# A fused attention and two-expert kernel: the second expert's first product by Strassen's scheme, the gain folded into its second weights, and the order of all steps made anew

## The chip, the cores and the metric

The kernel runs on one core of one Trainium2 chip. The metric is the device time of one execution in microseconds (us), lower is better. Before the change the median of three runs is 810.53 us (810.01 to 811.58).

## The reference

Three stages follow each other: causal attention for 4 batches of 8 heads (576 positions, 64 wide), then two feed-forward experts over the 2304 tokens that attention gives (model width 512).

```
cum  = cumsum(max(s, 0));  bias = -(cum[i] - cum[j])
scores = q @ k.T / sqrt(64);  scores = where(causal, -1e9, scores + min(bias, 0))
x  = softmax(scores) @ v                       # (2304, 512), heads side by side
h  = x @ w_in1;  g = h - tanh(h)               # expert 1: 512 -> 2048
x2 = g @ w_out1                                # 2048 -> 512
h  = x2 @ w_in2                                # expert 2: 512 -> 1024
e  = exp(h - max(h));  solu = h * e / (sum(e) + 1e-9)
ln = (solu - mean) / sqrt(var + 1e-6) * g_ln   # mean, var over the 1024 columns
out = ln @ w_out2                              # 1024 -> 512
```

## The kernel before

**Matrix products.** A float32 operand of the experts is split in two fp32r parts, a rounded one (hi) and the rest (lo), and each product is three matmuls on TensorE: hi x hi, lo x hi, hi x lo. A name that ends in h or l is such a part (`w2ih`, `w2il`). Weights arrive as 64-bit floats; `split_w` turns 512 columns of 128 rows into hi and lo: one load on SyncE's queue (tile `cd`), an absolute value (L408, ScalarE), four VectorE instructions (L390, L393, L396, L401), a cast for hi and a subtraction for lo (L312 on VectorE, L313 on GpSimd).

**Attention.** Work is cut into jobs by pair of heads; the first four pairs are cut again, into a head job (rows 1 to 4 of 64 positions) and the rest. A job loads k, q, v (`kn`, `q`, `v`) and the running sums of s (`bc`); in the head jobs `bc` is loaded as s itself, raised at zero and scanned by VectorE (L551), in the others it comes from DRAM (`cum_d`), where one scan for all pairs (L474) has been stored. Scores (L655), their mask (L663), a minimum with the bias that also gives the row's least value (L672, custom VectorE instruction, tile `U`), the exponential (L683, ScalarE), the division (L687, mostly GpSimd), transposes (L721), the weighted sum of v (L761), a store to DRAM (`xd`).

**Expert 1** runs on 9 blocks of 256 tokens by 16 chunks of 128 hidden columns: L808 gives h (12 matmuls of 256 columns), L813 tanh, L817 g, L831 the second product. Chunks 0 to 3 and 4 to 7 go first (`VISITS`), mixed into attention, with partial sums kept in DRAM (`pd`); chunks 8 to 15 use weights that replace attention's buffers once it is over (about 400 us).

**Expert 2** runs per tile of 128 tokens, 18 tiles, in `expert2`: h by 24 matmuls of 512 columns (L925: two halves of 512 columns, four slices of 128 of the 512 inputs, three matmuls each) into the two-bank PSUM tile `big`; its maximum (L930), the exponential (L934), sum, h times e (L942), mean and variance (L947, L951), centring and gain in one VectorE instruction (L954, scalar_tensor_tensor with the broadcast tile `gain`), Newton steps for the root (L967 to L969, GpSimd), transposes (L975), splits (L288, L982), 24 matmuls (L989) and the scaling of the output (L994).

**Order.** All steps are in a list, and `ORDER` is a table written by hand: each word is a step and the engine that does it, `+n` stands for n matmuls on junk data (L498) that keep TensorE busy. `Plan.order` replays the table; each engine's queue, SyncE's DMA queue among them, runs in that order. `BUFS` gives the number of buffers per tile name. In the last part PSUM holds two `big` tiles (four banks) and four single banks `t`.

## Time and profile before

| What | Value |
| --- | --- |
| median of three runs | 810.53 us (810.01 to 811.58) |
| the profiled execution, its own time | 813.61 us |
| its span in the trace | 811.8 us |
| TensorE matmuls busy | 790.6 us, 97% of the span |
| VectorE, ScalarE, GpSimd busy | 505.0, 382.8, 159.3 us (62%, 47%, 20%) |
| DMA engines, moved in all | 112.43 MB, mean 138 GB/s |

The profiled execution took 1.8 us more than its span (start and end outside the engines' records) and 3.1 us more than the median. Busy shares are means over parts with different limits; a stretch by itself tells more. Matmul records overlap one another, so the length of one is longer than its distance from the next.

### The profile page before, as it was taken

Reading aid. Unit: us, or ns where it says so; the run is one execution under the profiler, and the core shown is the slowest. Engines: PE = TensorE matmul, PEld = TensorE weight load, DVE = VectorE, ACT = ScalarE, POOL = GpSimd, SP = SyncE. Lnnn points to the kernel's source line nnn. Section 1 sums busy time; section 2 is a strip of 40 time slices with the busy share of each in tenths; the row PEclk is TensorE's granted clock in tenths of the full one; section 3 lists DMA queues with packets and bytes.
Section 4 is the critical chain, followed back from the end, with each engine's and each line's share of the span. In section 5 each row is a group of like instructions: output and inputs, shape, how many; then the busy total and the mean of one; then the engine's idle time right before and its main releaser. Section 6 shows DMA issues by size and latency. Waiting matters only on the chain.

```text
span 811.8 us, 16663 instructions
## 1 busy us (share of the span) xinstructions
PE 790.6 (97%) x6320; PEld 697.1 (86%) x6320; DVE 505.0 (62%) x1368; ACT 382.8 (47%) x973; POOL 159.3 (20%) x344
## 2 busy tenths in 40 slices
PE   7798999999999999999999999999999999999998
PEld 5457677788898999999999989899998889998886
DVE  5776688884454388865589875617364643245773
ACT  4786888886656355543355432313222222232222
POOL 3343333441223000000010012302142110001211
PEclk9999999999999999999999999999999999999999
DMA  7996897886653589785655501102020101100101
GB/s 204 258 275 163 266 259 215 258 234 199 176 165 95 170 298 288 227 267 161 227 159 182 157 27 66 40 14 79 27 79 14 52 24 61 36 1 14 40 13 52
DMA packets 89137, 112.43 MB, mean 138 GB/s; under 512 B 10768, under 2 KB 73232, under 8 KB 89056
## 3 DMA queue, kind: packets, MB, share of 16 engines
q1 hardware_dynamic: 89056, 111.35, 45.6%
q8 instruction: 50, 0.82, 0.4%
q14 instruction: 31, 0.25, 0.1%
HBM read 87.63 MB, written 23.70 MB: 137 GB/s over the span
## 4 chain that ended last, share of the span: by engine, by line
PE 74%; DMA 10%; DVE 10%; ACT 3%; issue 2%; SPq 1%; POOL 0%; ACTq 0%; DVEq 0%; POOLq 0%
PE t L808 17%; PE big L925 12%; PE t L989 12%; PE big L831 10%; PE acc L831 8%; PE t L761 5%; PE t L721 5%; PE t L655 4%; DMA cd<-in_moe_w_in_dram 4%; DMA cd<-in_moe_w_out_dram 2%; DMA bc<-cum_d 2%; PE t L975 2%; DVE ct L401 2%; DVE ct L396 2%; ACT ct L408 1%
## 5 line engine op out<-in xcount | busy, mean ns | idle before, releaser
L808 PE MATMUL t<-xb,wih 128*128 128x256 f32 x1152 | 206.5, 281 | 0.6 <-DVE g L817 0.6
L808 PEld LDWEIGHTS t<-xb,wih 128*128 128x128 f32 x1152 | 177.2, 189 | 1.9 <-DVE g L817 0.8
L808 PE MATMUL t<-xb,wil 128*128 128x256 f32 x576 | 161.0, 280 | 0.0
L687 POOL TENSOR_SCALAR U<-U,r 128x256 f32<-128x256 f32 (+8 forms) x144 | 81.2, 577 | 147.9 <-DVE r L599 83.0
L808 PEld LDWEIGHTS t<-xb,wil 128*128 128x128 f32 x576 | 109.5, 190 | 0.0
L831 PE MATMUL big<-gh,woh 128*128 128x256 f32 x576 | 104.5, 282 | 2.3 <-ACT gh L288 1.2
L831 PE MATMUL acc<-gh,woh 128*128 128x256 f32 x576 | 104.9, 283 | 1.2 <-DVE gh L312 0.6
L817 DVE TENSOR_TENSOR g<-t,th 128x256 f32<-128x256 f32 x144 | 59.7, 420 | 58.9 <-ACT th L813 53.9
L831 PEld LDWEIGHTS big<-gh,woh 128*128 128x128 f32 x576 | 88.9, 188 | 4.8 <-DVE gh L312 2.3
L683 ACT ACTIVATE U<-U,m 128x64 f32<-128x64 f32 (+8 forms) x144 | 80.3, 559 | 26.1 <-DVE m L672 25.4
L312 DVE TENSOR_TENSOR gh<-g,gh 128x256 fp32r<-128x256 f32 x122 | 54.0, 445 | 59.1 <-ACT gh L288 44.0
L288 ACT CAST gh<-g 128x256 fp32r<-128x256 f32 x141 | 56.5, 405 | 71.6 <-DVE g L817 34.0
L831 PEld LDWEIGHTS acc<-gh,woh 128*128 128x128 f32 x576 | 88.2, 189 | 2.4 <-issue 1.3
L813 ACT ACTIVATE th<-t 128x256 f32<-128x256 f32 x144 | 54.6, 382 | 75.0 <-PE t L808 60.2
L925 PE MATMUL big<-w2ih,x 128*128 128x512 f32 x288 | 89.8, 393 | 0.0
L831 PE MATMUL big<-gh,wol 128*128 128x256 f32 x288 | 80.6, 280 | 0.0
L831 PE MATMUL acc<-gh,wol 128*128 128x256 f32 x288 | 80.4, 279 | 0.0
L672 DVE CUSTOM_DVE_ANT_0 U<-bc,t 128x384 f32<-128x384 f32 (+8 forms) x144 | 59.4, 443 | 13.4 <-PE t L663 7.8
L288 ACT COPY pt<-t 128x512 f32<-128x512 f32 (+4 forms) x160 | 60.1, 429 | 6.8 <-PE t L721 6.1
L967 POOL TENSOR_SCALAR u<-y,va 128x1 f32<-128x1 f32 x51 | 25.7, 503 | 190.6 <-DVE y L962 186.9
L313 POOL TENSOR_TENSOR gh<-g,gh 128x256 fp32r<-128x256 f32 x22 | 16.8, 767 | 235.2 <-ACT gh L288 151.4
L655 PE MATMUL t<-kn,q 64*64 64x288 f32 (+8 forms) x640 | 59.1, 420 | 1.6 <-DMA q<-in_q_dram 0.7
(99 smaller groups left out, 1384.6 us busy)
## 6 DMA issues: line engine op xcount, KB each, us to landing
xb<-xd SPq DMA_DIRECT2D x17, 1024.0 KB, 6.2
cd<-in_moe_w_in_dram SPq DMA_DIRECT2D x24, 512.0 KB, 4.6
cd<-in_moe_w_out_dram SPq DMA_DIRECT2D x24, 512.0 KB, 4.1
bc<-cum_d SPq DMA_DIRECT2D x32, 288.0 KB, 5.7
pd<-xp SPq DMA_DIRECT2D x18, 512.0 KB, 4.1
xp<-pd SPq DMA_DIRECT2D x18, 512.0 KB, 3.7
xd<-xs SPq DMA_DIRECT2D x16, 320.0 KB, 4.5
kn<-in_k_dram SPq DMA_DIRECT2D x16, 288.0 KB, 5.1
```

Of the source, the lines that this page charges most:

```text
L288: nc.scalar.copy(o, i)
L312: return self.any([("dve", t_dve(n, pair=True), lambda: nc.vector.tensor_tensor(*views(), op), "diff-dve"), ("pool", t_pool(n), lambda: nc ...
L655: nc.tensor.matmul(X[a][c, :z - a], lhsT=V["q"][r, o:o + 64], rhs=V["k"][r, a:z], start=True, stop=True, skip_group_check=True)
L672: nc.vector.tensor_tensor_reduce(out=X["u"][:, a:z], in0=V["bc"][:, n, a:z], in1=X[b][:, a - b:z - b], scale=-0.125, scalar=X["m"] if "m" ...
L683: nc.scalar.activation(out=X["u"][:, :nk], in_=X["u"][:, :nk], func=AF.Exp, scale=-1.0, bias=X["m"], accum_out=Y["s"][:, n:n + 1])
L687: eng.tensor_scalar(X["u"][:, :nk], X["u"][:, :nk], Y["r"][:, n:n + 1], 1.0, ALU.mult, ALU.mult)
L808: nc.tensor.matmul(ps, lhsT=w[l][:, k, f * 128:f * 128 + 128], rhs=xb[:, r, k, :], start=k == 0 and x == 0, stop=k == 3 and x == 2)
L813: nc.scalar.activation(out=X["th", f], in_=X["h", f], func=AF.Tanh)
L817: nc.vector.tensor_tensor(X["g", f], X["h", f], X["th", f], ALU.subtract)
L831: nc.tensor.matmul(X["acc"][:, m, :], lhsT=w[l][:, f, m * 128:m * 128 + 128], rhs=X["gh", f][:, r, :], start=f == c0 and m % 2 == 0 and x ...
L925: nc.tensor.matmul(X["h"][:, n, :], lhsT=self.x2[j][:, l, k, 128 * o:128 * o + 128], rhs=r[:, k, 512 * n:512 * n + 512], start=k == 0 and ...
L989: nc.tensor.matmul(X["po"], lhsT=X["lt", k // 4][:, l, k % 4, :], rhs=r[:, k, :], start=k == 0 and a == 0, stop=k == 7 and a == 2)
```

## The change

1. `expert2`'s first product goes over to a new function `products`, per block of 256 tokens: the 2 x 2 halves of tokens, inputs and hidden columns are multiplied by Strassen's scheme, with 7 products of 6 matmuls (128x512) instead of 8. Sums of x halves are made in `split_x2`, sums of weight quarters in `load_w2i`; five VectorE instructions and two copies put the products together. For the second tile of a block the two last of them are custom instructions that also give the row's least value, and h stands negated in `hc` in SBUF. The bank `b` is a pool of its own (`pc`), so three banks `t` are left.
2. g_ln is multiplied into `w2_out` when it is converted (`load_w2o`, one pass more); centring is then a tensor_scalar without the broadcast tile.
3. One exponential on a single column stands first in ScalarE's queue (`table`).
4. More buffers for attention and conversion, a second `cd`; x tiles alternate between two pools; some waits at the switch to the last part name other steps.
5. `ORDER` is another table throughout.

```diff
-BUFS = dict(junk=1, U=7, ps=6, bc=3, kn=4, q=4, v=3, pt0=2, pt1=2, xs=2, xb=2, th=2, g=2, gh=3,
-            acc=1, h2=1, xp=1, cd=1, ct=2, cu=1, e=2, o=1, x2=1)
+BUFS = dict(junk=1, U=9, ps=6, bc=4, kn=5, q=5, v=4, pt0=2, pt1=2, xs=3, xb=2, th=2, g=2, gh=3,
+            acc=1, h2=1, hb=1, hc=1, u2=1, xp=1, cd=2, ct=2, cu=1, e=2, o=1, x2=1)
-c 0 x f 4l 31u 89 3 i r u 4f 4i 31x 320 46 323 6 7u m o +38 10 1r 326 2f 9 36 13 19 1u 17 329 1x 86 20 4a 1c bu 1f 2i
+0 f x 3 i 10 l u 49 7x p 4i r +22 13 4l 1u 16 2i 86 1a 1c 1x 39 bu 2l 20 2p 6 1f 23 2r 1i 3c 89 1l 2u 4d 26 2x bx 4f
...
+        def table():
+            nc.scalar.activation(out=self.small("y"), in_=self.one, func=AF.Exp)
+
+        add("act", 1600, table, [self.one_ready], ahead=1.0e6)
...
+        h1 = self.copy(lambda: (view(0, 0, 2).rearrange("p s k f -> p (s k) f"), f1()), 512, False, [c1])
...
+        t1 = less("t1", "b12", "b11", [c1, c2])
+        t2 = less("t2", "b22", "t1", [t1])
+        t3 = less("t3", "b22", "b12", [c2])
+        t4 = less("t4", "b21", "t2", [t2, c2])
+        h3 = self.copy(lambda: (view(0, 3, 5), pair(n1())), 512, False, [t2])
+        l3 = self.diff(lambda: (view(1, 3, 5), pair(n1()), bits(view(0, 3, 5))), 512, [h3, t4, l1], rel=("ct",))
...
+        s1 = self.diff(lambda: (a(1, 1), a(1, 0), a(1, 1)), 256, [lb], op=ALU.add, split=350.0)
+        s3 = self.diff(lambda: (a(1, 0), a(0, 0), a(1, 0)), 256, [s1], split=350.0)
+        s2 = self.diff(lambda: (a(0, 0), a(1, 1), a(0, 0)), 256, [s3, la], split=350.0)
+        s4 = self.diff(lambda: (a(0, 1), a(0, 1), a(0, 0)), 256, [s2], split=350.0)
+        hc = self.copy(lambda: (four(0), sums()), 1024, False, [s4])
+        lc = self.diff(lambda: (four(1), sums(), bits(four(0))), 1024, [hc], rel=("xp",))
...
+                for k in range(2):
+                    for n, (l, r) in enumerate(((0, self.w2ih), (1, self.w2ih), (0, self.w2il))):
+                        nc.tensor.matmul(o, lhsT=self.x2[j][:, l, x, k], rhs=r[:, b, k, :], start=start and k == 0 and n == 0,
+                                         stop=k == 1 and n == 2, skip_group_check=True)
...
+        p1 = pe(product(0, 0, 0, True, True), [la], ("h2",))
+        p6 = pe(product(3, 4, None, True, True), [lc], ("hb",))
+        p5 = pe(product(6, 3, 1, True, True), [lc])
+        k1 = self.copy(keep1, 512, True, [p1], acq=("hc",))
+        u2 = add("dve", t_dve(512), sum2, [k1, p6], acq=("u2",))
+        k5 = self.copy(lambda: (c(1), Z["h"][:, 1]), 512, True, [p5, k1])
+        u4 = add("dve", t_dve(512), lambda: nc.vector.tensor_tensor(Z["h"][:, 1, :], Z["h"][:, 1, :], Z["u"], ALU.add), [u2, k5],
+                 rel=("u2",))
+        k15 = self.diff(lambda: (c(1), c(1), c(0)), 512, [k1, k5], op=ALU.add)
+        p2 = pe(product(1, 1, 0, False, True), [k1, la])
+        p3 = pe(product(4, 2, 1, False, True), [u4])
+        p7 = pe(product(5, 5, None, False, True), [u2])
+        c22 = add("dve", t_dve(512) + 34, lambda: second(1), [p7, k15])
+        p4 = pe(product(2, 6, None, False, True), [c22, lb], rel=("x2",))
+        c21 = add("dve", t_dve(512) + 34, lambda: second(0), [p4], rel=("hb",))
...
-            nc.vector.scalar_tensor_tensor(out=X["e"], in0=X["e"], scalar=X["mv"][:, 0:1], in1=self.gain,
-                                           op0=ALU.subtract, op1=ALU.mult)
+            nc.vector.tensor_scalar(X["e"], X["e"], X["mv"][:, 0:1], 1.0, ALU.subtract, ALU.mult)
...
-            self.ps = e(tc.tile_pool(name="pb2", bufs=4, space=PSUM))
+            self.ps = e(tc.tile_pool(name="pb2", bufs=3, space=PSUM))
+            self.pc = e(tc.tile_pool(name="pc", bufs=1, space=PSUM))
```

What the new order does is read from the instruction lists of both kernels. First SyncE's DMA queue from its start (`cd` is a weight chunk, `pt` the s of all pairs, `cum_d` its stored running sum). Before:

```order
L528 DMA v<-in_v_dram 128x2x128 x2
L381 DMA cd<-in_moe_w_in_dram 128x4x256
L528 DMA v<-in_v_dram 128x2x128
L455 DMA pt_131<-in_s_dram 32x576
L539 DMA bc<-in_s_dram 64x256 x2
L520 DMA kn<-in_k_dram 128x256
L524 DMA q<-in_q_dram 128x256
```

After:

```order
L586 DMA q<-in_q_dram 128x256
L590 DMA v<-in_v_dram 128x2x128
L601 DMA bc<-in_s_dram 64x256 x2
L582 DMA kn<-in_k_dram 128x256
L601 DMA bc<-in_s_dram 64x256 x4
L582 DMA kn<-in_k_dram 128x256
```

The first pair of k and q is complete with the fifth issue instead of the ninth; the weight chunk and the s of all pairs have moved behind them.

Second, TensorE's list where the first step of expert 1 stands (junk matmuls are L498 before, L560 after; scores' mask L663 and L725; transposes L721 and L783). Before, behind some 30 us of listed attention work:

```order
L663 MATMUL t<-mask,unit_64 64x64
L498 LDWEIGHTS junk
L498 MATMUL acc<-junk 128x256
L721 MATMUL t<-idx,U 128x128 x4
L721 MATMUL t<-idx,U 64x128
L721 MATMUL t<-idx,U 128x128 x2
L721 MATMUL t<-idn,U 128x128
L808 MATMUL t<-xb,wih_92 128x256 x2
```

After:

```order
L725 MATMUL t<-mask,unit_102 64x64
L560 LDWEIGHTS junk
L560 MATMUL acc<-junk 128x256
L783 MATMUL t<-idn,U 128x128 x3
L870 MATMUL t<-xb,wih_93 128x256 x2
```

The first step of expert 1 (L808, now L870) has moved from row 402 of TensorE's list to row 213. Junk matmuls are 80 in all before, 38 of them ahead of the first score; after they are 49, 22 of them ahead of the first score.

Third, TensorE's list at the products of expert 2. Before, at the first tile, they follow one another without a step of another engine between them:

```order
L808 MATMUL t<-xb,wil_4787 128x256
L925 MATMUL big<-w2ih,x_6671 128x512 x2
L925 MATMUL big<-w2il,x_6671 128x512
L925 MATMUL big<-w2ih,x_6671 128x512 x2
L925 MATMUL big<-w2il,x_6671 128x512
```

After, at the second block's last two products (both into `b`, which VectorE's c22 reads between them; L1127 is the output product, L989 before):

```order
L1011 MATMUL b<-w2ih,x_7203 128x512 x2
L1011 MATMUL b<-w2il,x_7203 128x512
L1127 MATMUL t<-w2oh,cd 128x512 x2
L1127 MATMUL t<-w2ol,cd 128x512
L1127 MATMUL t<-w2oh,cd 128x512 x2
L1127 MATMUL t<-w2ol,cd 128x512
L1011 MATMUL b<-w2ih,x_7203 128x512 x2
L1011 MATMUL b<-w2il,x_7203 128x512
```

Six matmuls of another step stand between the two products here; in five of the nine blocks it is six of 512 or twelve of 256 columns, in the others more.

## Rows read from the trace of the kernel before

**Rows 1.** Stretches of the span: stretch, sum; then PE, PEld, DVE, ACT, POOL busy us (instructions), PE clock, DMA share, GB/s.

```profile
0.00:20.00 20.00, 15.86 (x149) 10.93 (x149) 12.10 (x62) 9.63 (x33) 6.54 (x24) 1.00 0.74 205
20.00:40.00 20.00, 15.37 (x150) 9.29 (x151) 15.64 (x62) 15.63 (x48) 6.87 (x11) 1.00 1.03 253
40.00:60.00 20.00, 19.53 (x198) 12.07 (x195) 15.75 (x70) 17.02 (x51) 9.14 (x15) 1.00 1.06 280
60.00:80.00 20.00, 17.83 (x153) 13.90 (x154) 13.30 (x47) 14.20 (x43) 7.77 (x14) 0.91 0.67 166
80.00:100.00 20.00, 18.63 (x210) 13.67 (x201) 14.86 (x66) 15.45 (x48) 7.61 (x14) 1.00 0.87 265
400.00:420.00 20.00, 18.11 (x154) 17.51 (x153) 17.47 (x38) 10.57 (x24) 1.25 (x2) 1.00 0.54 158
420.00:440.00 20.00, 19.57 (x162) 18.58 (x161) 18.85 (x38) 10.85 (x23) 1.07 (x1) 1.00 0.62 192
440.00:460.00 20.00, 19.36 (x171) 19.16 (x170) 17.29 (x33) 10.58 (x25) 2.49 (x2) 1.00 0.62 196
460.00:740.00 280.00, 280.00 (x1829) 255.89 (x1828) 141.93 (x268) 78.70 (x163) 46.81 (x125) 1.00 0.12 38
```

**Rows 2.** The chain that ended last, its pieces in order of time: start us, length us, what.

```profile
5.18 2.64 DMA q<-in_q_dram
21.49 8.65 DMA bc<-cum_d
...
779.53 5.44 PE big L925 x24
```

**Rows 3.** Groups of TensorE instructions, the whole span: busy us, mean ns, then idle before.

```profile
L925 PE MATMUL big<-w2ih,x 128*128 128x512 f32 x288 | 89.8, 393 | 0.0
```

**Rows 4.** SyncE's DMA issues from the start: start us, us, line, tile, count.

```profile
0.74 0.96 SPq L528 DMA_DIRECT2D v<-in_v_dram  x2
...
3.31 1.20 SPq L539 DMA_DIRECT2D bc<-in_s_dram  x2
...
5.18 0.43 SPq L524 DMA_DIRECT2D q<-in_q_dram  x1
```

**Rows 5.** TensorE from the start: start us, us, line, tiles, count, [idle before and releaser].

```profile
1.10 6.03 PE L498 MATMUL acc<-junk 128*128 128x256 bf16 x38 [1.10 <-POOL junk L493]
7.87 0.33 PE L655 MATMUL t<-kn,q 64*64 64x64 f32 x4 [0.75 <-DMA q<-in_q_dram]
```

**Rows 6.** VectorE and ScalarE from the start, same columns.

```profile
7.99 1.35 DVE L474 TENSOR_TENSOR_SCAN pt<-one,pt 32x576 f32<-32x576 f32 x1
9.27 0.65 DVE L551 TENSOR_TENSOR_SCAN bc<-one,bc 128x256 f32<-128x256 f32 x1
10.43 0.20 DVE L672 CUSTOM_DVE_ANT_0 U<-bc,t 128x64 f32<-128x64 f32 x1
...
0.73 1.28 ACT L408 ACT_TABLE_LOAD   x1 [0.73 <-PEq L1144]
7.25 0.42 ACT L545 ACTIVATE bc<-bc 128x256 f32<-128x256 f32 x1 [0.57 <-DMA bc<-in_s_dram]
```

**Rows 7.** What TensorE waited for, 0 to 100 us: total us, times, longest us.

```profile
PE t L721 <- POOL U L687: 6.5, 7, 2.2
```

**Rows 8.** TensorE around 34 us and from 61 us, columns as in rows 5.

```profile
34.42 1.70 PE L498 MATMUL acc<-junk 128*128 128x256 bf16 x14
...
61.16 0.48 PE L808 MATMUL t<-xb,wih 128*128 128x256 f32 x2
```

**Rows 9.** Groups of VectorE and ScalarE instructions, by form: busy us, mean ns | idle before.

```profile
L954 DVE SCALAR_TENSOR_TENSOR ct<-ct,mv,gain 128x1024 f32<-128x1024 f32 x18 | 23.1, 1281 | 0.3
L390 DVE TENSOR_SCALAR ct<-ct 128x512 f32<-128x512 f32 x6 | 2.7, 443 | 1.1 <-ACT ct L408 1.1
...
L672 DVE CUSTOM_DVE_ANT_0 U<-bc,t 128x512 f32<-128x512 f32 x16 | 10.8, 672 | 0.7 <-PE t L663 0.3 <-PE t L655 0.2
...
L288 ACT COPY pt<-t 128x512 f32<-128x512 f32 x48 | 27.7, 590 | 2.9 <-PE t L721 2.6
```

More of the change, by code (lines that the diff above doesn't have):

```diff
@@ L341, in setup @@
         self.st.tile([128, 16], F32, name="pad_st", bufs=1)
+        self.gain = self.st.tile([128, 8], F32, name="gain", bufs=1)
         self.wes = ExitStack()
+        self.xo = self.wes.enter_context(tc.tile_pool(name="xo", bufs=1, side="left"))
         self.wa = self.w1_tiles(self.wes.enter_context(tc.tile_pool(name="wa", bufs=1, side="left")), 0, FA)
@@ L415, in split_w @@
                      [d], acq=("ct",))
+        if turn:
+            self.chain(turn + "d", d)
+            self.chain(turn, a)
         c = a
@@ L837, in expert1 @@
         else:
-            ld = self.dma(128 * 8192, load, list(ready), acq=("xb",), ahead=T["xb"],
+            ld = self.dma(128 * 8192, load, list(ready) + (list(deps) if j else []), acq=("xb",), ahead=T["xb"],
                           cost=650.0 * (1 + (j * TB // self.S != (j * TB + TB - 1) // self.S)))
@@ new lines, in split_x2, with first @@
+        two = lambda l: at(l, 0, 2).rearrange("p s k t -> p (s k) t")
+        four = lambda l: at(l, 3, 7).rearrange("p (r c) k t -> p r (c k) t", r=2)
+        sums = lambda: X["xp"].rearrange("p k (r t) -> p r k t", r=2)
+        def first():
+            self.x2[j] = self.sb(self.wl, [128, 2, 7, 2, 128], "x2", F32R)
+            return two(0), X["xp"][:, :, 0:128]
+        s = self.join(j, X, s)
+        ha = self.copy(first, 512, False, [s], acq=("x2",))
+        hb = self.copy(lambda: (at(0, 2, 3)[:, 0], a(1, 1)), 256, False, [s, ha])
@@ L915, in expert2 @@
+    def expert2(self, t, Z):
         nc, add = self.nc, self.add
@@ L994, in fin @@
             nc.scalar.activation(out=X["o"], in_=X["po"], func=AF.Copy, scale=X["y"])
-        for n in range(2):
-            for k in (0, 2):
-                s = add("pe", t_pe(1360.0, 3072), lambda n=n, k=k: h2(n, k), [x2s] + [self.w2_ready[4 * n + c] for c in range(4)],
-                        acq=("h2",) if n == k == 0 else (), rel=("x2",) if o and n and k else ())
-                s.after = [self.h2_last] if self.h2_last else []
-                self.h2_last = s
-        s = add("dve", t_dve(1024), top, [s])
-        s = add("act", t_act(1024, True, 2), expo, [s] + list(self.w2_ready.values()), acq=("ct",))
+        s = Z["steps"][o]
+        if not o:
+            s = add("dve", t_dve(1024), top, [s])
+        s = add("act", t_act(1024, not o, 2), expo, [s] + list(self.w2_ready.values()), acq=("ct",))
         s = add("dve", 271, inverse, [s])
         s.lag = 11.0
-        s = add("dve", t_dve(1024) + 65, solu, [s], rel=("h2",))
+        s = add("dve", t_dve(1024) + 65, solu, [s], rel=("hc" if o else "h2",))
         for n in range(2):
```

385 lines of the change are left out of this document (226 added, 159 removed).

## The prediction

> **What bounds the kernel now.** I read the stretches of the span first [rows 1]: columns are busy time per engine. From 460 to 740 us TensorE is busy 280.00 of 280.00 us, VectorE 141.93 (51%), the DMA engines 12%. There TensorE alone sets the pace, and a matmul less is time less. It is not so at two other places. In the first 100 us TensorE is idle 4.1, 4.6, 0.5, 2.2 and 1.4 us per 20 us, the DMA engines are full from 20 to 60 us (share 1.03 and 1.06), and from 60 to 80 us the granted clock is 0.91, a mean over its two levels. From 400 to 460 us TensorE lacks 3.0 us of 60, with VectorE busy 53.6: the weights of the last part are converted there. Then the chain that ended last [rows 2]: it begins with the first load of q and goes through a load of `bc`, which tells that the start waits for DMA; later it is made of matmuls, L925 among them. The waits of TensorE [rows 7] name what is late in the first 100 us: seven waits, 6.5 us, for GpSimd's division L687. The timelines of the first 11 us [rows 4 to 6] give the start step by step.
>
> **The change, term by term.** The sum is made against the profiled execution, 813.6 us (span 811.8, and 1.8 outside it). It lies 3.1 above the median of 810.5, and I take 3.1 off at the end.
>
> *Strassen's products.* Before, 18 tiles of 24 matmuls are 432; after, 9 blocks of 7 products of 6 matmuls are 378, so 54 go. The 393 ns of a group row [rows 3] is not what one costs, since matmuls overlap; the chain has 24 in 5.44 us [rows 2], 0.227 us each. 54 x 0.227 = **-12.2**. All stand where TensorE is full, so nothing else hides it. The Trainium skill, TensorE: Matmul & The Clock Gate, section Back-to-back issue gap, gives about 131 ns per matmul of 512 columns in a sustained stream of load and multiply; by that estimate the term would be 54 x 0.131 = 7.1 us and the whole would come out 5.1 us later. The trace disagrees, with 227 ns, and the measured spacing stands in my sum.
>
> *The start.* Before, q is issued at 5.18 us behind v, a weight chunk and s [rows 4] and has landed 2.64 us later [rows 2], and the first score runs at 7.87 [rows 5]. In the new list q, v and two `bc` issues stand ahead of the first k. With 0.43 for a q, half of 0.96 for a v and 1.20 for two `bc`, that k is issued at 0.74 + 0.43 + 0.48 + 1.20 = 2.85 us and lands, with the same 2.64, at 5.5. But VectorE is what the scores then meet: its first minimum runs at 10.43, behind the scan L551 at 9.27, which stood behind the scan of all pairs L474 (7.99, 1.35 us long) [rows 6]. In the new list L474 and the weight conversion stand behind the first minima. `bc` is issued at 1.65 instead of 3.31 [rows 4], so its rise, which ended at 7.25 + 0.42 = 7.67 [rows 6], ends at 6.0, the scan of 0.65 at 6.7, and the minimum comes 10.43 - 6.7 = **-3.7** earlier. Ends: 0, if the DMA engines that it hurries to are full a little later anyway [rows 1], and -3.7.
>
> *The rest of the first 100 us.* What can be seen as lost behind the first score: idle time 4.1 less the 1.85 before it [rows 5], 4.6, 0.5, 2.2 and 1.4, in sum 10.9 [rows 1], and 42 junk matmuls, which stand where nothing else is ready, 14 of them in 1.70 us [rows 8], 0.12 each, 5.1 in sum: 16.0 us. The new list has expert 1's first step at row 213 of TensorE instead of 402, which stood at 61.16 us [rows 8]; that gives TensorE work to do while GpSimd is late [rows 7], and more buffers let loads start earlier. Nothing in the trace prices this. The nearest measure is the junk in the list, since it stands where the order has no real work: 27 behind the first score instead of 42, a share of 0.36 less. 0.36 x 16.0 = **-5.7**. Ends: 0, because the DMA engines are full from 20 to 60 us and the same bytes must come, and -16.0.
>
> *400 to 460 us.* At most the 3.0 us that TensorE lacks there can be won [rows 1]. The conversion grows: per quarter of the weights four subtractions of 256 columns and splits of 768 columns more, 1792 columns or 3.5 instructions of 512, four quarters; at 0.67 us, that of a two-input VectorE instruction of 512 columns [rows 9], 9.4 us. VectorE has 6.4 us free in that stretch, so 3.0 us could show. Ends -3.0 and +3.0, and I take **0**. GpSimd may take some of it, and the one further pass for g_ln is on ScalarE, busy 10.6 of 20 us [rows 1]; VectorE covers neither if it is full.
>
> *Waits inside the products.* Before, none: 24 matmuls follow one another. Now the last product of a block must wait for c22, which reads the bank `b` that it writes. In five of nine blocks only one group of matmuls stands between, 6 x 0.227 = 1.36 us. c22 takes 0.67 by the nearest custom instruction [rows 9]; if VectorE has just begun one of 1.28 us (L954's kind), 1.95, and TensorE stands 0.59 us. Ends 0 and 5 x 0.59 = 3.0; I take the middle, **+1.5**. Other products have 2.2 us and more between them and their VectorE step.
>
> *Work beside it, nothing.* Five VectorE instructions of 512 columns per block (9 x 5 x 0.67 = 30 us), as much again at most for sums and wider splits of x, less two centrings per block (1.28 before; 2 x 0.443 = 0.89 by L390, or still 1.28 [rows 9]): 23 to 60 us, say 40, over some 350 us. VectorE goes from 51% to about 62%, and TensorE covers it. Two copies of 0.59 per block [rows 9] are ScalarE's, which is idle there for most of the time. If the cover is gone, that is the third rival. The early table load gains nothing: the load stands at 0.73 us already, and ScalarE next works after 6 us [rows 6]. The end is left alone: the last blocks' products and the last output product stand as before.
>
> Sum: 813.6 - 12.2 - 3.7 - 5.7 + 0 + 1.5 = 793.5, less 3.1: **790.4 us**.
>
> **The rivals.**
>
> First, *only the products pay*: the early part is set by DMA. For it: share 1.03 and 1.06 from 20 to 60 us, and the chain runs through an 8.65 us load of `bc` [rows 1, 2]. Against it: the wait rows name GpSimd, not a DMA [rows 7], and work that needs no load (expert 1 on x of the first heads) now stands earlier. 813.6 - 12.2 + 1.5 - 3.1 = **799.8**.
>
> Second, *three banks instead of four*: each of the 72 steps of expert 1 in the last part takes a bank `t` and gives it back when other engines have read it. If every third finds none and waits for one reading of 512 columns, 0.59 us [rows 9], that is 24 x 0.59 = 14.2: **804.6**. Against it: a group of 12 matmuls takes longer than that reading, and the step before it is already one bank ahead. The Trainium skill, Perfetto Trace Analysis, section on the optimization strategy, says that the same gap repeating on the engine that should be saturated can mean too few buffers in SBUF or PSUM; no row of before shows such gaps, and it is this rival's mark.
>
> Third, on the other side, *VectorE sets the pace of the products*. Its place is the chain inside a block: three products wait for a VectorE step (p3, p7, p4). If each meets a copy of 0.59, an instruction of 1.28 ahead in VectorE's queue and its own 0.67 [rows 9], 2.54 us less 1.36 of cover is 1.18; 27 x 1.18 = 31.9 in place of my 1.5: **820.8**, slower. From (810.5 - 790.4) / 1.18, 17 of the 27 waits, it is no gain. That needs VectorE at 80% and more, where the rows and the extra work give 62%.
>
> **How the numbers follow.** Forecast 0.65, first rival 0.20, second 0.06, third 0.05 (with 0.01 of it near no change); 0.04 for more than my terms at the start. The range reaches up to the first rival with part of the 3.0 us of the conversion (801) and down to where most of the 16.0 us goes, 790.4 - 10.3 = 780: **780 to 801**. A measurement of this kernel can tell about 0.2%, 1.6 us. All cases but the third rival are faster by more: 0.95; within 0.2%: 0.01; slower: 0.04.
>
> **What would show it.** Right: 378 matmuls of the first product, 24 of them in 5.4 to 5.5 us; first score near 5.5 us and first minimum near 6.7; the first step of expert 1 far before 61 us; less idle time and no clock below 1.00 in the first 100 us; VectorE near 62% from 460 to 740 us with TensorE still full. Wrong: idle time of TensorE at the products, ended by c22 or the sums of VectorE; the same small gap ahead of expert 1's steps, ended by tanh or g (banks); a wait for `bc` or x that takes the early gain back; or TensorE lacking more than 3.0 us from 400 to 460 us.

## The result, and the profile after

The changed kernel takes **797.48 us** (median of 4 runs, 796.89 to 798.65), the kernel before on the same chip 811.06 us (4 runs, 810.01 to 811.63). The ratio is 0.9836, 95% interval 0.9819 to 0.9853: 13.6 us or 1.6% less. Forecast were 790.4 us and a range from 780 to 801. The sign and the range held; the time is 7.1 us longer than forecast. The profiled execution took 797.47 us (span 795.7), which is the median, so nothing has to be taken off here.

The stretches of the span of the kernel after, columns as in [rows 1]:

```profile
0.00:20.00 20.00, 16.49 (x156) 10.98 (x156) 12.31 (x77) 12.30 (x45) 8.72 (x28) 1.00 0.66 176
20.00:40.00 20.00, 17.21 (x165) 11.17 (x165) 16.01 (x58) 15.39 (x45) 6.69 (x10) 1.00 1.02 303
40.00:60.00 20.00, 18.96 (x175) 13.57 (x173) 16.73 (x54) 14.88 (x38) 6.32 (x8) 1.00 1.07 283
60.00:80.00 20.00, 18.47 (x193) 11.48 (x194) 15.73 (x72) 18.38 (x59) 9.96 (x17) 1.00 0.99 255
80.00:100.00 20.00, 19.74 (x210) 15.66 (x209) 18.37 (x76) 18.00 (x58) 8.16 (x13) 1.00 1.07 334
400.00:420.00 20.00, 19.83 (x174) 19.64 (x174) 19.07 (x42) 11.61 (x26) 0.90 (x1) 1.00 0.42 135
420.00:440.00 20.00, 20.00 (x175) 19.91 (x174) 19.73 (x46) 11.30 (x26) 0.74 (x1) 1.00 0.51 155
440.00:460.00 20.00, 18.70 (x123) 16.84 (x123) 19.03 (x39) 11.62 (x25) 1.52 (x1) 1.00 0.47 159
460.00:740.00 280.00, 276.48 (x1832) 249.33 (x1832) 178.77 (x387) 101.09 (x205) 47.48 (x124) 1.00 0.15 48
```

Three things stand out against [rows 1]. The hole of the DMA engines at 60 to 80 us (0.67) has been filled (0.99). The granted clock there is 1.00 instead of 0.91, but that is not the change's doing: in b_pad, the kernel before with its tiles shifted by 32 bytes (below), the clock is 1.00 there too, with the same hole (0.64). VectorE goes from 51% to 64% in the last stretch (178.77 of 280; forecast 62%). And TensorE, which was busy for all of the 280 us, now lacks 3.5 of them.

TensorE's waits of the kernel after from 100 us on, the three largest (total us, times, longest us):

```profile
PE big L1011 <- DVE big L1042: 5.0, 6, 1.3
PE acc L893 <- ACT ct L419: 0.9, 1, 0.9
PE big L893 <- DVE xp L955: 0.6, 1, 0.6
```

The first is new: a Strassen product (L1011) stands six times for u4 (L1042), 5.0 us in all. The names are those of the code: p1 to p7 are the products of a block; u4 is VectorE's sum in the half of the tile `big` that p5 has written and to which p3 is added next; k15 is VectorE's sum of the copies of p1 and p5. The seven waits for GpSimd at the start [rows 7], 6.5 us, are four and 1.3 us now (L749). In all TensorE is idle for 9.1 us of the first 100, where it was 12.8 [rows 1].

**How far ahead it is, and where.** A steady measure is how many matmuls of expert 1 are done at a given time; at 400 us attention is over in both kernels. Groups by line up to 400 us that differ, first of the kernel before, then of the one after (x is the count):

```profile
L808 PE MATMUL t<-xb,wih 128*128 128x256 f32 x616 | 111.2, 283 | 0.0
L808 PE MATMUL t<-xb,wil 128*128 128x256 f32 x307 | 85.9, 280 | 0.0
L831 PE MATMUL big<-gh,woh 128*128 128x256 f32 x24 | 4.3, 281 | 0.0
L831 PE MATMUL big<-gh,wol 128*128 128x256 f32 x12 | 3.4, 281 | 0.0
```

```profile
L870 PE MATMUL t<-xb,wih 128*128 128x256 f32 x640 | 116.4, 283 | 0.1
L870 PE MATMUL t<-xb,wil 128*128 128x256 f32 x320 | 89.9, 281 | 0.0
L893 PE MATMUL big<-gh,woh 128*128 128x256 f32 x36 | 6.2, 276 | 0.0
L893 PE MATMUL big<-gh,wol 128*128 128x256 f32 x18 | 5.0, 276 | 0.0
```

That is 1014 against 959, 55 more. At 0.117 us each (5.63 us for 48 in the chain, shown further down) the kernel after is **6.4 us ahead at 400 us**. Part of this belongs to the profiled execution of before, which took 3.1 us more than its median: b_pad's, which lies near its own median, has done 969 by then, 10 more than before. At 460 us both have done 2303 of expert 1, and the kernel after 42 matmuls of the products as well: 42 x 0.227 = 9.5 us ahead, so 400 to 460 us gave 3.1 us. From 460 us to the end of its span it takes 335.7 us instead of 351.8 (795.7 - 460 and 811.8 - 460), 16.1 us less. It has 42 + 54 = 96 fewer matmuls of 512 columns to do there, worth 96 x 0.227 = 21.8 us. So **5.7 us were lost again behind 460 us**; five of the six waits for u4 stand there, 3.7 us.

The start of the kernel after, columns as in [rows 4 to 6], of SyncE, TensorE and VectorE:

```profile
2.90 0.59 SPq L582 DMA_DIRECT2D kn<-in_k_dram  x1
...
5.76 0.33 PE L717 MATMUL t<-kn,q 64*64 64x64 f32 x4
...
6.61 0.22 DVE L734 CUSTOM_DVE_ANT_0 U<-bc,t 128x64 f32<-128x64 f32 x1 [0.15 <-DVE bc L613]
```

and, later on TensorE, the first step of expert 1:

```profile
31.47 0.50 PE L870 MATMUL t<-xb,wih 128*128 128x256 f32 x2
```

The issue was forecast at 2.85, the score at 5.5, the minimum at 6.7 us; they stand at 2.90, 5.76 and 6.61. The first step of expert 1 was at 61.16 [rows 8] and is at 31.47.

### The profile page after: what moved, and what is told of

Its sections match the earlier page's. It is cut to its first block, busy times and chain, and to the rows that moved or that the text cites. A ratio compares the mean times of both kernels' runs of the same rounds, so it can differ in the third digit from the quotient of the medians.

```text
span 795.7 us, 16621 instructions
## 1 busy us (share of the span) xinstructions
PE 775.7 (97%) x6235; PEld 683.5 (86%) x6235; DVE 542.2 (68%) x1521; ACT 413.0 (52%) x1028; POOL 155.7 (20%) x321
## 4 chain that ended last, share of the span: by engine, by line
PE 76%; DVE 12%; ACT 5%; DMA 3%; issue 2%; SPq 1%; POOL 0%; ACTq 0%; DVEq 0%; POOLq 0%
PE t L870 19%; PE t L1127 12%; PE acc L893 11%; PE big L893 9%; PE big L1011 6%; PE t L823 5%; PE b L1011 4%; PE t L783 4%; PE t L717 4%; PE t L1113 2%; DMA cd<-in_moe_w_out_dram 2%; DVE ct L407 1%; DVE ct L412 1%; DVE U L734 1%; DVE g L879 1%
## 5 line engine op out<-in xcount | busy, mean ns | idle before, releaser
L870 PE MATMUL t<-xb,wih 128*128 128x256 f32 x1152 | 205.7, 281 | 0.3 <-DVE g L879 0.2
L870 PEld LDWEIGHTS t<-xb,wih 128*128 128x128 f32 x1152 | 176.8, 189 | 2.4 <-DVE g L879 0.4
L870 PE MATMUL t<-xb,wil 128*128 128x256 f32 x576 | 160.7, 279 | 0.0
L749 POOL TENSOR_SCALAR U<-U,r 128x256 f32<-128x256 f32 (+8 forms) x144 | 85.6, 606 | 177.1 <-DVE r L661 68.7
L870 PEld LDWEIGHTS t<-xb,wil 128*128 128x128 f32 x576 | 108.6, 188 | 0.0
L893 PE MATMUL acc<-gh,woh 128*128 128x256 f32 x576 | 105.3, 283 | 0.9 <-ACT ct L419 0.9
L893 PE MATMUL big<-gh,woh 128*128 128x256 f32 x576 | 100.7, 278 | 0.6 <-DVE xp L955 0.6
L745 ACT ACTIVATE U<-U,m 128x256 f32<-128x256 f32 (+8 forms) x144 | 80.2, 559 | 19.1 <-DVE m L734 18.5
L893 PEld LDWEIGHTS acc<-gh,woh 128*128 128x128 f32 x576 | 88.1, 189 | 2.2 <-ACT th L875 1.1
L893 PEld LDWEIGHTS big<-gh,woh 128*128 128x128 f32 x576 | 87.8, 188 | 1.8 <-ACT th L875 0.7
L317 DVE TENSOR_TENSOR gh<-g,gh 128x256 fp32r<-128x256 f32 x130 | 56.1, 434 | 38.5 <-ACT gh L293 38.1
L893 PE MATMUL acc<-gh,wol 128*128 128x256 f32 x288 | 80.8, 280 | 0.2 <-DVE wol L317 0.2
L893 PE MATMUL big<-gh,wol 128*128 128x256 f32 x288 | 79.7, 277 | 0.0
L734 DVE CUSTOM_DVE_ANT_0 U<-bc,t 128x256 f32<-128x256 f32 (+8 forms) x144 | 60.1, 441 | 6.4 <-PE t L725 3.0
L893 PEld LDWEIGHTS acc<-gh,wol 128*128 128x128 f32 x288 | 54.2, 188 | 0.4 <-DVE wol L317 0.4
L893 PEld LDWEIGHTS big<-gh,wol 128*128 128x128 f32 x288 | 54.1, 188 | 0.0
L823 PE MATMUL t<-pt,v 128*64 128x320 f32 (+4 forms) x448 | 52.2, 366 | 1.6 <-DVE m L734 1.3
```

Source lines behind the costliest of these rows:

```text
L317: return self.any([("dve", t_dve(n, pair=True), lambda: nc.vector.tensor_tensor(*views(), op), "diff-dve"), ("pool", t_pool(n) + split, la ...
L734: nc.vector.tensor_tensor_reduce(out=X["u"][:, a:z], in0=V["bc"][:, n, a:z], in1=X[b][:, a - b:z - b], scale=-0.125, scalar=X["m"] if "m" ...
L745: nc.scalar.activation(out=X["u"][:, :nk], in_=X["u"][:, :nk], func=AF.Exp, scale=-1.0, bias=X["m"], accum_out=Y["s"][:, n:n + 1])
L749: eng.tensor_scalar(X["u"][:, :nk], X["u"][:, :nk], Y["r"][:, n:n + 1], 1.0, ALU.mult, ALU.mult)
L823: nc.tensor.matmul(X["x"][r, q0:gw], lhsT=V["v"][:kc, c, r], rhs=V["pt", g][:kc, cc, h, r0:r0 + gw - q0], start=c == 0, stop=c == len(part ...
L870: nc.tensor.matmul(ps, lhsT=w[l][:, k, f * 128:f * 128 + 128], rhs=xb[:, r, k, :], start=k == 0 and x == 0, stop=k == 3 and x == 2)
```

## The experiments

Each kernel was run beside the kernel before on one chip. That one took 811.50 us on the chip of the first four, 812.76 on that of the second four, 810.83 on that of a_best, a_dma and a_stt, and 812.59 on that of a_dma2; its single executions there lie between 808.1 and 817.8. So a difference of 2 us between kernels that ran on two chips may be the chips'. In the diffs `-` is the changed kernel, unless another is named.

### First four: addresses, one late product, the price of a product

Steps of expert 1 take other times per matmul in the two kernels, although they are the same instructions. One thing that differs is where tiles start in SBUF: the weights of expert 1 that are used up to 400 us start at 224 modulo 256 bytes before, and at 0 after the change, which put a tile of 32 bytes (`gain`, 8 columns) ahead of them. A pad tile stands there as well; its size shifts everything behind it in that part of SBUF: these weights, every second x tile up to 400 us, and later the tiles of the second expert's weights and x (`w2`, `x2`). The weights of chunks 8 to 15 and the other tiles of expert 1 do not move.

**a_pad** shifts them on by 32 bytes:

```diff
-        self.st.tile([128, 16], F32, name="pad_st", bufs=1)
+        self.st.tile([128, 24], F32, name="pad_st", bufs=1)
```

> The changed kernel with 32 bytes more of padding ahead of the pools wa, wl and xo: their tiles then start at 32 bytes past a multiple of 64 in each partition, where the change had put them on a multiple of 64 (in the kernel before they were at 32 too). Nothing else differs. Theory of the addresses: in the changed kernel's trace a matmul of 256 columns follows the last after 117.2 ns where the weights lie on a multiple of 64 and 120.0 where the moving operand does too, and after 113.3 in the chunks 8 to 15, whose weights lie at 32; the 512-column ones take 233.3 (L1127) and about 230 (L1011) against 226.7 before the change. With everything at 32: 432 x 6.7 + 432 x 3.9 (L870, first half) + 864 x 3.9 (L893, first half) + 432 x 6.7 (L1127) + 378 x 3.3 ns (L1011) = 12.2 us less, about 785.5 us, and 113.3 and 226.7 ns throughout. Rival: the spacing comes from what the other engines and the DMAs do meanwhile, or differs by chance between the two profiled runs: no change, 797.5 us.

Measured: 800.12 us (798.58 to 800.63; ratio 0.9852, 0.9826 to 0.9879), not faster at all. In its chain a step of 48 takes 5.70 us, 119 ns a matmul, where the kernel after has 5.63:

```profile
325.07 5.70 PE acc L893 x48
```

The theory in that form fell. The spacing did move with the pad, but both ways: 48 early matmuls take longer, the output product (L1127) 5.50 us for 24 instead of 5.60, and the steps of expert 1 in the last part, whose own tiles the pad does not move, 5.65 us for 48 instead of 5.44:

```profile
498.57 5.50 PE t L1127 x24
...
642.68 5.65 PE t L870 x48
```

**b_pad** is the same edit in the kernel before (16 to 24), which puts its weights where the change has them.

> The kernel before with the same 32 bytes of padding: its wa and wl tiles move from 32 past a multiple of 64 onto a multiple of 64, as in the changed kernel. Theory of the addresses: up to 1728 x 3.9 (first half of expert 1) + 432 x 6.7 (L989) + 432 x 3.3 ns (L925) = 11.0 us more, about 821 us, with 117.2 ns at 256 columns where the trace of before has 113.4; less, to 5 us, as far as before already has stretches at 117.8 ns. Rival, chance or other engines: 811 us.

Measured: 812.56 us (810.94 to 816.18; ratio 1.0013, 0.9991 to 1.0034): no difference. Its chain says why the sum is nothing: steps of expert 1 are longer in the first half (5.70 us for 48, where the kernel before has 5.44 at one place and 5.65 at others) and shorter in the last part (5.46 where it has 5.65), while the 24 of the output product (L989) take 5.60 instead of 5.44. The kernel before first, then b_pad:

```profile
261.95 5.44 PE t L808 x48
...
377.67 5.65 PE t L808 x48
```

```profile
260.04 5.70 PE t L808 x48
...
376.49 5.70 PE t L808 x48
```

So effects of both signs can cancel in the total. This run also points to the 3.1 us by which the profiled execution of before lay above its median as that execution's own: here the profile (812.97) is 0.4 above its median, with the clock at 1.00.

**a_p3** puts the product p3, which adds to u4's sum, later, behind p7 or the next step, in every block where it stood; here in TensorE's instruction list at the first block:

```
+L1011 MATMUL b<-w2ih,x_6571 128x512 x2
+L1011 MATMUL b<-w2il,x_6571 128x512
+L1011 MATMUL b<-w2ih,x_6571 128x512 x2
+L1011 MATMUL b<-w2il,x_6571 128x512
 L1011 MATMUL big<-w2ih,x_6571 128x512 x2
 L1011 MATMUL big<-w2il,x_6571 128x512
 L1011 MATMUL big<-w2ih,x_6571 128x512 x2
 L1011 MATMUL big<-w2il,x_6571 128x512
-L1011 MATMUL b<-w2ih,x_6571 128x512 x2
-L1011 MATMUL b<-w2il,x_6571 128x512
-L1011 MATMUL b<-w2ih,x_6571 128x512 x2
-L1011 MATMUL b<-w2il,x_6571 128x512
```

> The changed kernel with product p3 later in TensorE's list: behind p7 where the two are neighbours, behind the next other step in the two blocks where they are not. p3 is the product that waits for VectorE's u4 (six waits, 5.0 us in the changed kernel's trace). Theory: the wait is only too little work between p5 and p3; with 1.4 us or more between them it goes, 3.5 to 5.0 us faster, about 793 us. Rival: VectorE is late as such, the wait moves to p4 behind c22 or to the tile's maximum, and the time stays at 797.5.

Measured: 801.86 us (800.03 to 805.08; ratio 0.9886, 0.9858 to 0.9913), slower than the change itself. TensorE's waits of a_p3 from 100 us on (its lines stand two lower):

```profile
PE big L893 <- DVE xp L955: 2.9, 2, 1.9
PE b L1011 <- DVE m L1029: 2.1, 4, 0.5
PE t L1125 <- DVE cu L1118: 1.4, 1, 1.4
PE t L1111 <- DVE ct L1091: 0.9, 2, 0.6
```

The waits for u4 are gone, and 7.3 us of others stand there: for c22 (L1029), for the sum that closes a block of expert 1 (L955, of which 0.6 us stood in the kernel after too) and for steps behind the products (L1118, L1091). The rival's mechanism came: the waits moved on. The time is 4 us worse than it said, and the waits, 2 us more in sum than in the kernel after, account for half of that. Moving the product that waits does not pay.

**a_x8** does the first of the seven products twice, so that a block has eight; the second result takes the place of the first.

```diff
-                for k in range(2):
+                for k in (0, 1, 0, 1) if x == 0 else (0, 1):
```

> The changed kernel with its first product computed twice in each block (the second result takes the place of the first): 54 matmuls of 512 columns more, 432 as in the kernel before. Theory: TensorE sets the pace and each is worth its spacing of 0.227 to 0.230 us: 12.2 to 12.4 us slower, about 809.8. Rival: by now VectorE's chain sets the pace in the last part, and a good part of the added work disappears in waits: less than 8 us slower.

Measured: 808.39 us (807.23 to 810.83; ratio 0.996, 0.9945 to 0.9975). Against the repeat of the change below, on another chip, the median is 10.2 us longer; with each taken against the kernel before on its own chip it is 11.4 (3.1 us and 14.5 us less than that). The profiled spans differ by 809.0 - 796.4 = 12.6, but a_x8's is that of its slowest execution. The products have 54 matmuls more, 36 of them in this group (144 after the change), 18 in that of the low part:

```profile
L1011 PE MATMUL big<-w2ih,x 128*128 128x512 f32 x180 | 57.1, 398 | 4.3 <-DVE big L1042 4.3
```

By the medians a product's matmul is worth 0.19 to 0.21 us, and by the spans 0.233. The time lies 1.4 us below the expected 809.8 and far from the rival's: the term of 12.2 us is about right, at the upper end of what was measured.

### Second four: repeat, start, u4, addresses again

**a_same** is the changed kernel once more, on the chip of the next three.

> The changed kernel once more, unchanged, so that its variants of this call stand beside it on one chip. Every theory: 797.5 us within 1.5; its profile again has about 5 us of waits for VectorE's u4 at the products and its first score near 5.8 us.

Measured: 798.23 us (796.25 to 800.43; ratio 0.9813, 0.9788 to 0.9839), with the wait for u4 at 5.1 us. Its matmuls of expert 1 by 400 us are 1877 (after: 1878), so this count repeats.

**a_start** moves the first issue of q back behind v, a weight chunk, the s of all pairs, four `bc` and a k (the top of SyncE's list):

```
-L586 DMA q<-in_q_dram 128x256
 L590 DMA v<-in_v_dram 128x2x128
-L601 DMA bc<-in_s_dram 64x256 x2
-L582 DMA kn<-in_k_dram 128x256
+L392 DMA cd<-in_moe_w_in_dram 128x4x256
+L512 DMA pt_116<-in_s_dram 32x576
```

> The changed kernel with the first DMA issues in nearly the old order: a v, the first weight chunk, the s of all pairs and four bc stand ahead of the first k and q, so that q is issued at about 5.2 us, as in the kernel before, instead of 0.74; nothing else is moved. Theory of the start: the first score comes 2.1 us later and the first minimum 1.6, and as TensorE has little else to do there, 1.6 to 2.1 us reach the end: 799.3 us. Rival (the early gain is lost where the DMA engines are full, 20 to 100 us): the loads behind it keep their order, nothing reaches the end, 797.5.

Measured: 798.37 us (796.62 to 798.76; ratio 0.9809, 0.9788 to 0.9831): the same as a_same. The first score of a_start, and its first two stretches of 10 us:

```profile
8.03 0.48 PE L717 MATMUL t<-kn,q 64*64 64x64 f32 x4 [2.98 <-DMA q<-in_q_dram]
```

```profile
0.00:10.00 10.00, 5.92 (x42) 4.36 (x44) 1.47 (x8) 2.84 (x7) 2.22 (x14) 0.87 0.64 173
10.00:20.00 10.00, 10.00 (x100) 6.63 (x98) 9.25 (x57) 6.93 (x29) 4.54 (x10) 0.79 0.55 146
```

The first score was made 2.3 us later (8.03 against 5.76), the first minimum 2.0 (8.63 against 6.61), with a lower clock on top. By 40 us TensorE has done 311 matmuls of all kinds against 316 in a_same, by 400 us 3703 and 3702. The rival's time came: what this edit takes away does not reach the end. It undoes only 2.0 of the 3.8 us by which the change had brought the first minimum forward, and in exchange the first weight chunk is issued at 1.24 us instead of 11.04; what that alone is worth was not separated.

**a_p2** puts p2 ahead of p5 and u4 ahead of k15, in each block where they stood otherwise. VectorE's and TensorE's lists at the second block (lines two lower, the transposes L1113 are L1111):

```
+L1040 TENSOR_TENSOR big<-big,u_7091 128x512
 L317 TENSOR_TENSOR hc<-hc 128x512
-L1042 TENSOR_TENSOR big<-big,u_7085 128x512
```

```
-L1113 MATMUL t<-idn,ct 128x128 x12
 L1011 MATMUL big<-w2ih,x_7203 128x512 x2
 L1011 MATMUL big<-w2il,x_7203 128x512
 L1011 MATMUL big<-w2ih,x_7203 128x512 x2
 L1011 MATMUL big<-w2il,x_7203 128x512
+L1111 MATMUL t<-idn,ct 128x128 x12
```

The reason is in the timeline of the kernel after, at the second block:

```profile
520.46 0.39 PE L1011 MATMUL big<-w2il,x 128*128 128x512 f32 x1
...
520.89 0.59 ACT L293 COPY hc<-big 128x512 f32<-128x512 f32 x1 [2.06 <-PE big L1011]
...
521.51 0.69 DVE L317 TENSOR_TENSOR hc<-hc 128x512 f32<-128x512 f32 x1 [1.29 <-ACT hc L293]
...
522.78 0.39 PE L1011 MATMUL big<-w2il,x 128*128 128x512 f32 x1
...
523.21 0.70 DVE L1042 TENSOR_TENSOR big<-big,u 128x512 f32<-128x512 f32 x1 [1.01 <-PE big L1011]
...
523.96 0.74 PE L1011 MATMUL big<-w2ih,x 128*128 128x512 f32 x2 [0.79 <-DVE big L1042]
```

p5, to whose half of `big` u4 adds, ends at 520.85, the copy of it at 521.48. VectorE is free at 522.20. But u4 starts at 523.21, when p2 has ended (522.78 + 0.39), and p2 writes the *other* half of `big`. Both halves are one tile, and p2 stands ahead of u4 in the program, so u4 waits for a result that it does not read. Then p3, behind it, finds TensorE standing for 0.79 us.

That is so in three of the six waits (0.79 us each, 2.4 in all). In the other three (1.30, 0.64 and 0.64 us) p2 does not stand there; k15, which stands ahead of u4 in VectorE's queue, does, and u4 follows it without a gap. At the fourth block:

```profile
567.61 0.69 DVE L317 TENSOR_TENSOR hc<-hc 128x512 f32<-128x512 f32 x1 [1.52 <-ACT hc L293]
...
568.22 0.69 DVE L1042 TENSOR_TENSOR big<-big,u 128x512 f32<-128x512 f32 x1
...
568.97 0.72 PE L1011 MATMUL big<-w2ih,x 128*128 128x512 f32 x2 [0.64 <-DVE big L1042]
```

The two halves of the edit answer these two cases.

> The changed kernel with product p2 ahead of p5 in TensorE's list (behind p6 or what follows it) and u4 ahead of k15 in VectorE's. In the changed kernel u4 waits for p2 to end, since both work on the tile big and p2 stands between p5 and u4 in the order in which the program is written: in the second block's trace VectorE is idle 0.95 us until p2 ends, adds for 0.70 us, and p3 waits 0.79. Theory of this wait: with p2 ahead, u4 runs while TensorE does the step between, the six waits shrink from 5.0 to under 2 us, and 3 to 4 us come off: 793.5 to 794.5 us. Rival (VectorE late as such, as when p3 was moved): the waits move to c22 and to the tile's maximum and the time is 797.5 or more.

Measured: 794.67 us (793.3 to 795.86; ratio 0.9768, 0.9747 to 0.979), 3.6 below a_same. What is left of the wait in a_p2, from 100 us on:

```profile
PE big L1011 <- DVE big L1040: 1.1, 2, 0.5
```

From 5.1 to 1.1 us of wait, and 3.6 us of time (its slowest execution is below the fastest of a_same): the theory held, and this part of the loss is a price of the order, not of VectorE's load. What p2 and what k15 costs by itself was not run. By the waits, all of k15's 2.6 us are gone; the 1.1 us that are left stand in two of p2's three blocks.

**a_pad8** shifts the same tiles the other way, which puts them at 224 modulo 256, where the weights stood before the change.

```diff
-        self.st.tile([128, 16], F32, name="pad_st", bufs=1)
+        self.st.tile([128, 8], F32, name="pad_st", bufs=1)
```

> The changed kernel with 32 bytes less of padding ahead of the pools wa, wl and xo: their tiles start at 224 past a multiple of 256, as all weights did in the kernel before (with 32 bytes more they were at 32, and expert 1's first half stayed at 120 ns). Theory of the addresses: the first half's steps go from 117.2 and 120 to the 113.4 to 117.8 ns of the kernel before, the 512-column matmuls from 233.3 and 230 to 226.7: 1728 x 3 ns + 432 x 6.7 ns + 378 x 3.3 ns, up to 9 us less; as the last part's expert 1 may get the 117.8 that the kernel before has there, 4 to 9 us faster, 788.5 to 793.5. Rival: the spacing doesn't go with the addresses, or what one kind of step wins another loses: 796 to 799.

Measured: 794.36 us (793.62 to 796.1; ratio 0.9768, 0.9746 to 0.979), 3.9 below a_same, again without overlap of the four executions; the direction as expected, the size just short of it. Groups up to 400 us of a_pad8 where it differs from the kernel after:

```profile
L893 PE MATMUL big<-gh,woh 128*128 128x256 f32 x58 | 10.0, 276 | 0.0
L893 PE MATMUL big<-gh,wol 128*128 128x256 f32 x28 | 7.7, 276 | 0.0
```

That is 86 instead of 54, 32 x 0.117 = 3.7 us more done by 400 us: in sum all of the gain lies there. Where it comes from is seen in the chains, steps of the same length, first the kernel after, then a_pad8 (start us, length us, what, count):

```profile
323.78 5.63 PE acc L893 x48
...
496.36 5.60 PE t L1127 x24
...
668.02 5.44 PE t L870 x48
```

```profile
352.03 5.46 PE acc L893 x48
...
492.85 5.45 PE t L1127 x24
...
636.30 5.65 PE t L870 x48
```

117.3 ns a matmul become 113.8 before 400 us, and 233 ns become 227 in the output product. In the last part it is the reverse for expert 1, 113.3 against 117.7.

### The rest: both together, the DMA engines, VectorE's cover

**a_best** is a_p2 with a_pad8's edit.

> Both edits that gained, together: product p2 ahead of p5 and u4 ahead of k15, and 32 bytes less of padding (weights at 224 past a multiple of 256). If they are independent, as one takes away waits of TensorE and the other shortens the distance of matmuls, 3.6 + 3.9 us come off the changed kernel's 798.2: 790.7 us. Rival: the shorter distance only opened waits that the other takes away too: 794.

Measured: 791.94 us (790.31 to 793.63; ratio 0.9756, 0.9731 to 0.9781). It has the shortest time here, 2.4 us below a_pad8, where a_p2's edit alone was worth 3.6. But it ran on another chip, on which the kernel before was faster too (810.83 us here, 812.76 there); by the ratio to that one, 0.9756 against 0.9768 for a_p2 and for a_pad8, the intervals overlap for the most part. That it beats either is not shown, nor whether the two gains add.

**a_dma** loads the first four weight chunks twice into the same tile, to price DMA work in the first 100 us.

```diff
-            nc.sync.dma_start(out=d.rearrange("p a b -> p (a b)") if len(shape) == 2 else
-                              d.rearrange("p (k f) b -> p k (f b)", k=shape[1]), in_=src)
+            self.loads = getattr(self, "loads", 0) + 1
+            for _ in range(2 if self.loads <= 4 else 1):
+                nc.sync.dma_start(out=d.rearrange("p a b -> p (a b)") if len(shape) == 2 else
+                                  d.rearrange("p (k f) b -> p k (f b)", k=shape[1]), in_=src)
```

> The changed kernel with the first four weight chunks loaded twice (each a second time into the same tile, right behind the first): 2.1 MB more between 11 and 40 us. Theory: the first 100 us are set by the DMA engines, whose share in the changed kernel's trace is 0.93 to 1.08 in every 10 us from 20 to 100, so that the early start is lost there; 2.1 MB at some 300 GB/s are 7 us, and 4 to 7 us reach the end: 802 to 805 us. Rival: VectorE, ScalarE and GpSimd set that part and the loads run ahead: less than 1.5 us, 797 to 799.5.

Measured: 813.54 us (812.54 to 816.87; ratio 1.0032, 1.0015 to 1.005), far beyond both. The edit did more than it should: the second load into a tile waited for the first, on SyncE's queue, with every later issue behind it:

```profile
25.22 7.55 SPq L394 DMA_DIRECT2D cd<-in_moe_w_out_dram  x2
```

So it priced a held queue, not bytes: four such pairs, 5.4 to 7.6 us each on the queue, cost 15 us at the end. It says that this queue is on the path of the early part, and nothing on the bytes.

**a_dma2** copies the same four chunks to spare DRAM tiles, so that nothing waits for the copies.

```diff
+            self.loads = getattr(self, "loads", 0) + 1
+            if self.loads <= 4:
+                x = self.dr.tile([128, 1024], I32, name=f"extra{self.loads}")
+                nc.sync.dma_start(out=x if len(shape) == 2 else x.rearrange("p (k f) -> p k f", k=shape[1]), in_=src)
```

> The changed kernel with the first four weight chunks also copied once to spare tiles in DRAM, which nothing reads: 2.1 MB more read (and written to DRAM) for the DMA engines between 11 and 45 us, without a step that waits for them and without the second load into the same tile that held SyncE's queue for some 6.5 us each time in the run before. Theory: the DMA engines, full from 20 to 100 us, set that part; 2.1 MB at some 300 GB/s are 7 us, of which 4 to 7 reach the end: 801.5 to 805 us. Rival: not their bandwidth but the order and the waits of SyncE's queue and the engines' steps set it: under 1.5 us, below 799.5.

Measured: 800.6 us (800.14 to 801.36; ratio 0.9864, 0.9835 to 0.9893), 2.4 us above a_same, which ran on another chip: between the two expectations. At 400 us its profiled execution has done 14 matmuls of expert 1 fewer (1863 against 1877), 1.6 us. Inconclusive: the edit costs something here, but less than the full time of its bytes, and it adds four issues to SyncE's queue as well.

**a_stt** makes the centring of the rows (L1093) a two-input VectorE instruction again, with ones as second input.

```diff
-            nc.vector.tensor_scalar(X["e"], X["e"], X["mv"][:, 0:1], 1.0, ALU.subtract, ALU.mult)
+            nc.vector.scalar_tensor_tensor(out=X["e"].rearrange("p a b -> p (a b)"), in0=X["e"].rearrange("p a b -> p (a b)"),
+                                           scalar=X["mv"][:, 0:1], in1=self.one.to_broadcast([128, 1024]), op0=ALU.subtract, op1=ALU.mult)
```

> The changed kernel with its centring put back to a two-input VectorE instruction (scalar_tensor_tensor, with a broadcast column of ones as the second input): 1.28 us instead of about 0.74, 18 times, 9.7 us more for VectorE in the last part. Theory: VectorE has room there (64% busy from 460 to 740 us) and TensorE covers it: 797.5 to 799.5 us. Rival: the products' waits on VectorE grow by what lies ahead of u4 and c22 in its queue: 801 or more.

Measured: 800.54 us (799.68 to 802.84; ratio 0.9863, 0.9837 to 0.9889), 2.3 us above a_same, on another chip; against the kernel before on each chip it is 4.2 us. It lies between the two expectations. The instruction takes 1278 ns instead of 746, 18 times, 9.6 us more of VectorE. First its group in the kernel after, then a new wait of TensorE in a_stt:

```profile
L1093 DVE TENSOR_SCALAR ct<-ct,mv 128x1024 f32<-128x1024 f32 x18 | 13.4, 746 | 0.1
```

```profile
PE t L1114 <- DVE ct L1093: 1.3, 2, 0.9
```

Its profiled execution (span 800.4) is 4.0 us longer than that of a_same (796.4). At 400 us, where this edit does nothing, it was 10 matmuls of expert 1 behind (1867 against 1877, 1.2 us), so 2.8 us came later, 1.3 of them in the new wait. TensorE covers part of VectorE's extra 9.6 us, but not all: 2 to 4 us come through.

Not tried: the deeper buffers of the early part alone. The new order needs them, so they can't be put back under it. Nor was the early exponential taken out.

## Why the prediction was right in sign and 7.1 us off

The range held because the largest term was right. Term by term:

- *Strassen's products*, -12.2: **right**. 378 matmuls are left, and a_x8, the reverse, gave 10.2 to 11.4 us by the medians. The spacing here is 0.227 to 0.233 us. The estimate by the Trainium skill, TensorE: Matmul & The Clock Gate, section Back-to-back issue gap, of 131 ns and 7.1 us, fits neither.
- *The start*, -3.7: the working was right to 0.3 us at each step (2.90, 5.76 and 6.61 against 2.85, 5.5 and 6.7), the worth was wrong. It is **0** at the end as far as a_start tells, which undoes 2.0 of the 3.8 us and brings a weight chunk forward for it. That is the lower end of its bounds; whether the reason given there, full DMA engines, is the right one was not shown.
- *The rest of the first 100 us*, -5.7: **too small**, by about what the start was too large. With the addresses of before (a_pad8) the kernel is 55 + 32 = 87 matmuls of expert 1 ahead at 400 us, 10.2 us, where start and rest together had 9.4; up to 3.1 us of it may be the longer execution of before. That the two misses cancel is luck. Here too, GpSimd's waits went from 6.5 to 1.3 us, and the DMA engines' hole at 60 to 80 us was filled.

  From 20 to 100 us, 20 us x (253 + 280 + 166 + 265) GB/s = 19.3 MB were moved before [rows 1], 20 us x (303 + 283 + 255 + 334) GB/s = 23.5 MB after. Whether the buffers or the earlier steps of expert 1 did it wasn't separated.
- *400 to 460 us*, 0: gained 3.1 us, at the end of -3.0. The conversion's extra work did not show, though VectorE is busy 57.8 of the 60 us.
- *Waits inside the products*, +1.5 (0 to 3.0): **mis-sized, and the first step that failed**. Measured 5.0 us, and at another place: not p4 behind c22 (no idle time stands ahead of the products into `b`), but p3 behind u4. The sentence that failed is "Other products have 2.2 us and more between them and their VectorE step". In three blocks one step of twelve matmuls stands between p5 and p3, 1.4 us, and a copy (0.59), k15 (0.69) and u4 (0.69) do not fit into it. In the other three some 2.3 us stand there, but u4 starts late, behind a product that it does not read. a_p2 gives 3.6 us back.
- *Work beside it, nothing*: nearly. VectorE 64% instead of 62%, the centring 746 ns where 886 or 1281 were taken, and 9.6 us more of it cost 2 to 4 us (a_stt), so the cover is not whole.
- **Not in the sum at all**, and the second step that failed: matmuls that the change leaves alone were taken at their old price. It had moved tiles by 32 bytes, and moving them back is worth 3.9 us (a_pad8).
- *The 3.1 us taken off at the end*: they look like that execution's own (b_pad). But what was lost in it, with the clock at 60 to 80 us low, can stand in the 16.0 us of idle time as well, and then part of it was taken off twice.

The waits (5.0 - 1.5 = 3.5) and the address (3.9) make 7.4 us, about the 7.1 that were missed. The other misses nearly cancel: start +3.7, rest -4.5 (10.2 - 5.7), 400 to 460 us -3.1, and up to 3.1 taken off twice. This is bookkeeping over single executions, which differ by 1 to 2 us; that it closes does not show that nothing else was missed.

The rivals. *Only the products pay* (799.8) comes near by its number and not by its reason: by 400 us the kernel is 6.4 us ahead. *Three banks instead of four*: no row of after shows a repeated gap ahead of L870, the largest wait there is 0.2 us. *VectorE sets the pace* did not happen, yet its mechanism, a chain inside a block, is what u4's wait is, six times instead of seventeen.

## What to carry to other kernels

When a product is split over the halves of one tile, ask of each reader which writers stand ahead of it in the program, not only which half it reads, and what else stands ahead of it in its engine's queue. Here the cure was the order of these steps (two tiles were not tried), and moving the waiting product back only handed the wait on. Before counting an earlier start as a gain, look how much of the lead is left some tens of us later. When a change adds or moves small tiles, compare the spacing of untouched matmuls before and after: an unchanged instruction can cost 3% more, here 3.9 us in all.
